# One row table with whole rows for chunks 0 to 7, its first read free of the later scatters, and counts in four steps a phase

## The chip, the core and the metric

The kernel runs on one core of a Trainium2 chip. The metric is the time of one execution in microseconds (us) on the device, the median over several runs. A profiled execution gives the trace; its own time and its span are in the table below.

## What is computed

Three stages follow one another on 1536 tokens of 512 features: a linear attention with decay, a dense MLP, and a mixture of eight experts. The change touches the last one, whose routing gives every token to exactly one expert, with at most 192 tokens an expert:

```python
cap = N // E                      # 1536 // 8 = 192
order = np.argsort(-(x @ w_gate).flatten())
for idx in order:                 # best (token, expert) pair first
    tok, e = divmod(int(idx), E)
    if assigned[tok] >= 0 or counts[e] >= cap:
        continue
    assigned[tok] = e; counts[e] += 1
for e in range(E):
    mask = assigned == e
    out[mask] = np.maximum(x[mask] @ w1[e], 0.0) @ w2[e]
```

## The kernel before

**Tiling.** The tokens are 12 chunks of 128. A product in float32 quality is three fp16 products of high and low parts. TensorE (PE) computes the MLP's second product `x2p` chunk by chunk (L647): 48 matmuls a chunk, 512 columns wide for chunks 0 to 7 and 384 wide for chunks 8 to 11. The last 128 columns of chunks 8 to 11 come later in one piece, `x2q` (L682), and are turned back by PE transposes `x2t` (L691).

**Routing** needs no x2, only logits, and runs beside that work. It takes seven phases (loop from L759). In a phase PE transposes the tokens' current best logits into a row of 1536 values (L767), ACT copies it to SBUF (L769), and for every chunk i a 0/1 matrix G (128 tokens by 1536) says which tokens are ahead of which: VectorE (DVE) writes the part left of the diagonal (L800) and the part right of it (L809); for chunks 8 to 11 ACT writes the left part in two passes (L803, L806). PE then counts with 32-column weights, four matmuls of 384 columns side by side for a chunk (`count`, L825 to L829, matmuls at L828): two chunks in a step, six steps a phase, in the order 0 1, 2 11, 3 4, 10 5, 9 6, 8 7. Ahead of the last step twelve `ties` matmuls (L792) use the same 32-column weights; their 0/1 inputs come from GpSimd (POOL, L775, L777) and DVE (L782). DVE thresholds the counts (L839), PE sums flags (L846, L847), and DVE settles the phase and makes the next logits (L737 to L752).

**Rows out and back in.** After the phases DVE writes every token's slot `pos` (L865). POOL scatters the x2 rows to DRAM, sorted by expert, with indirect DMAs, each of 128 rows: 12 into `xsa` (768 fp16 values a row, features 0 to 383 as high and low parts) and 12 into `xsb` (288 values a row: features 384 to 511, then the token's number and zeros); all at L881. Three of the `xsb` scatters stand among the first 12, nine behind them. A `memset` of a spare word (L879) separates scatters into one table. The SBUF copies are `xa` (three tiles of four chunks, pool B) and `xb` (one tile, pool B; a copy and a memset on POOL, L667 and L668, write the numbers and zeros). SP then reads the rows of two experts at a time with transposing DMAs, `xs<-xsa` (L903) and `xs<-xsb` (L904), and the numbers with four small DMAs (L909, L910). PE's first expert product `hp` (L928) takes features 0 to 383 of experts 0 and 1 first and their last 128 features after that; `po` (L958) is the second product.

**Order.** `Plan` writes the order by hand: `add` gives a step an engine, a planned cost, what it waits for, its buffers and a key; `run` (L96) simulates five engines and a shared DMA with these costs and emits the steps in the order of planned time, the lowest key first among those ready. So each engine's order is fixed ahead, and `x2p` matmuls (each a step of its own) fill PE wherever nothing with a lower key is ready in the plan. On the chip an engine runs its list in that order and waits where the data is late. Pool B has 21 buffers of 8 KB a partition, H has 2 of 4 KB, and the G tiles of chunks 8 to 11 take their buffers from H. Loads of expert weights (`ws`, L981) go through SP too, behind the row reads in its list.

Of the kernel before, what the change touches and what calls it, by code (L numbers as in the profile page):

```python
# [26 lines left out]
XA = 768  # L27
XB = 288
# [20 lines left out]
class Plan:  # L49
# [16 lines left out]
    def buf(self, pool, shape, dt, name):  # L66
        return Buf(self, pool, shape, dt, name)
# [28 lines left out]
    def run(self):  # L96
# [14 lines left out]
        while avail:  # L111
# [81 lines left out]
def fused_kernel(ctx, tc, raw_d, lam_d, win_d, wout_d, wg_d, w1_d, w2_d, out):  # L193
# [23 lines left out]
    def C(shape, dt, name):  # L217
        return cst.tile(shape, dt, name=name)
# [417 lines left out]
    xbb = buf("B", [P, NCH, XB], F16, "xb")  # L636

    def x2_part(j, d0, d1, pool, key):
        n = d1 - d0
        ps = buf(pool, [P, n // P, P], F32, f"x2p{j}_{d0}")  # L640
        prev = None
        for fc in range(16):
            w, w_done = wout[fc // 4]

            for y, z in ((0, 0), (0, 1), (1, 0)):
                def mm(fc=fc, w=w, y=y, z=z):
                    te.matmul(ps[:], gsl(y, fc, j), w[:, z, fc % 4, d0:d1], start=(fc + y + z == 0), stop=(fc == 15 and y == 1))  # L647
# [3 lines left out]
        parts = ([(xab[j // 4], t_xa, d0 // P, a)] if d0 < 384 else []) + ([(xbb, t_xb, b - 3, 1)] if d1 > 384 else [])  # L651
        if n == 512:
            parts = [(xab[j // 4], t_xa, 0, 3), (xbb, t_xb, 0, 1)]
        k0 = 0
        for x, done, ka, kb in parts:
            def v(y, x=x, ka=ka, kb=kb):
                return x[:, j if x is xbb else j % 4, 2 * P * ka:2 * P * kb].rearrange("p (k y d) -> p y k d", y=2, d=P)[:, y]
            src = slice(k0, k0 + kb - ka)
            k0 += kb - ka
            sc = 2.0 ** -9 / 6.0  # L660
            h = add("se", c_se((kb - ka) * P), lambda v=v, src=src: se.activation(v(0), ps[:, src], AF.Copy, scale=sc), [prev], [x, ps], key)
            lo = add("ve", c_ve((kb - ka) * P), lambda v=v, src=src: ve.scalar_tensor_tensor(
                v(1), ps[:, src], sc, v(0), op0=OP.mult, op1=OP.subtract), [h], [x, ps], key)
            done[j] = [lo]
            if x is xbb and j == 0:
                def tail():
                    ge.tensor_copy(xbb[:, :, 256:258].bitcast(I32), ids.unsqueeze(2))  # L667
                    ge.memset(xbb[:, :, 258:], 0.0)  # L668
                ids_in.append(add("ge", 0.4, tail, [prev], [x], key))
    for j in range(NCH):  # L670
        if j % 4 == 0:
            xab[j // 4] = buf("B", [P, 4, XA], F16, f"xa_{j}")
        x2_part(j, 0, 512 if j < JB else 384, "pB" if j % 3 == 2 else "pC", x_key + 11 * j)

    def x2_rest(b, key):
# [17 lines left out]
        r = slice(4 * b, 4 * b + 4)  # L693
        h = add("se", c_se(512), lambda: se.activation(xbb[:, r, 0:P], pt[:], AF.Copy), [t], [xbb, pt], GK)
        lo = add("ve", c_ve(512), lambda: ve.tensor_tensor(xbb[:, r, P:2 * P], pt[:], xbb[:, r, 0:P], op=OP.subtract), [h], [xbb, pt], GK)
        for j in range(4 * b, 4 * b + 4):
            t_xb[j] = [lo]
    x2_rest(2, x_key + 11 * NCH + 24)
    t_x2 = [t_xb[j] if j < JB else t_xa[j] for j in range(NCH)]

# [13 lines left out]
    pos = C([P, NCH], I32, "pos")  # L714
# [5 lines left out]
    BY_GE = 8  # L720

# [37 lines left out]
    for p in range(PHASES):  # L759
# [33 lines left out]
        order_c = [0, 1, 2, 11, 3, 4, 10, 5, 9, 6, 8, 7]  # L793
        group, t_g = [], []
        for n, i in enumerate(order_c):
# [26 lines left out]
            if len(group) < 2:  # L822
                continue

            def count(group=group, n=n, cp=cp):  # L825
                for i, z, G in group:
                    for k in range(4):
                        te.matmul(cp[32 * k:32 * k + 32, :], ohc[:, i], G[:, z, 384 * k:384 * k + 384], start=(n == 1 and i == group[0][0]),  # L828
                                  stop=(n == NCH - 1 and i == group[1][0]))  # L829
# [45 lines left out]
    last_to = []  # L875

    def scatter(dst, idx, src, done):
        if last_to[-1:] == [id(done)]:
            ge.memset(spare, 0.0)  # L879
        last_to.append(id(done))  # L880
        s = ge.indirect_dma_start(out=dst, out_offset=bass.IndirectOffsetOnAxis(ap=idx, axis=0), in_=src, in_offset=None)  # L881
        for o in done:
            tc.declare_no_dep(s.ins, o.ins, reason="distinct rows")
        done.append(s)
    sca, scb = [], []
    t_sa = [add("ge", 1.28, lambda j=j: scatter(xsa_d[:, :], pos[:, j:j + 1], xab[j // 4][:, j % 4], sca),
                [t_pos] + t_xa[j], [xab[j // 4]], GK + j, 0, 2 * P * XA) for j in range(NCH)]

    t_sb = [add("ge", 1.28, lambda j=j: scatter(xsb_d[:, :], pos[:, j:j + 1], xbb[:, j], scb),
                [t_pos] + t_xb[j] + ids_in + ([t_sa[3 * j + 2]] if j < 3 else t_sa[-1:]), [xbb], GK + (3 * j + 2.5 if j < 3 else NCH + j), 0, 2 * P * XB)  # L890
# [4 lines left out]
    xs, t_xs = {}, {}  # L895
    h1, t_h1 = {}, {}
    l1_first = {}

    def experts_in(q, key):
        xs[q] = buf("B", [P, 8, 2 * CAP], F16, f"xs{q}")  # L900
        r = slice(2 * CAP * q, 2 * CAP * q + 2 * CAP)
        first = [l1_first[2 * q - 2]] if q else []
        t_xs[q] = [add("sp", 4.7 if q else 2.4, lambda: sy.dma_start_transpose(out=xs[q][:, 0:6], in_=xsa_d[r, :]), t_sa + first, [xs[q]], key, 0, 725000),  # L903
                   add("sp", 1.25, lambda: sy.dma_start_transpose(out=xs[q][:, 6:8], in_=xsb_d[r, 0:256]), t_sb + first, [xs[q]], key, 0, 242000)]  # L904

    def load_rows():
        v = xsb_d[:, 256:258].bitcast(I32).rearrange("(q z c) o -> z c q o", z=2, c=CAP)
# [140 lines left out]
```

## Time and profile before

| | |
|---|---|
| median of 3 runs | 508.85 us (508.14 to 509.87) |
| the profiled execution | 508.18 us, span 506.3 us |
| mean granted TensorE clock | 0.992 of full speed |
| PE busy | 484.0 us, 96% of the span |
| DVE, ACT, POOL busy | 398.6, 309.1, 166.4 us |

Times in the rows below are microseconds from the span's start. The 2 us between the profiled execution's time and its span lie outside the first and last instruction. A row of a timeline reads: start, duration, engine, line of the kernel, operation, written tile and what it is made from, shape, how many merged, and in brackets the idle time of the engine just before and what ended it. Neighbouring matmuls overlap in the pipeline, so the time that one costs is read from start to start.

### The profile page before, as it was taken

The numbers are of one execution on the slowest core, as the hardware profiler recorded it, in microseconds if no ns is written. First come the engines' busy times: TensorE is split into PE (matmuls) and PEld (weight loads), VectorE is DVE, ScalarE is ACT, GpSimd is POOL, SyncE is SP. The second block draws the span as 40 slices with busy tenths as digits, with TensorE's granted clock in tenths as the row PEclk, the third lists the DMA queues.
The fourth block names the chain that finished last, engine by engine and source line by source line (L and its number), as shares of the span: only waits on it lengthen the run. The fifth ranks groups of instructions, "written<-read, shape, count | busy, mean of one in ns | idle before, by whom it ended". The sixth has DMA issues, their size and how long they took to land.

```text
span 506.3 us, 10304 instructions
## 1 busy us (share of the span) xinstructions
PE 484.0 (96%) x4241; PEld 294.2 (58%) x4243; DVE 398.6 (79%) x707; ACT 309.1 (61%) x486; POOL 166.4 (33%) x167
## 2 busy tenths in 40 slices
PE   8779998999999999999999999999999999999995
PEld 3467554787785444534434434546577685776862
DVE  7699999988688886598899889887644797989620
ACT  1586959764546664286687568574523758687510
POOL 2022334020222220076257347436880232323201
PEclk9898999999999999999999999999999999999999
DMA  7999426220264541000000000655665999998011
GB/s 225 398 415 411 179 84 247 85 43 2 84 250 85 99 89 22 2 2 1 1 1 2 1 0 1 250 201 189 225 142 176 370 285 423 320 399 358 1 43 41
DMA packets 44910, 77.86 MB, mean 154 GB/s; under 512 B 33080, under 2 KB 34112, under 8 KB 38720
## 3 DMA queue, kind: packets, MB, share of 16 engines
q1 hardware_dynamic: 42752, 70.82, 41.5%
q0 software_dynamic: 2112, 6.39, 3.4%
q8 instruction: 33, 0.54, 0.4%
q14 instruction: 13, 0.11, 0.1%
HBM read 63.46 MB, written 6.40 MB: 138 GB/s over the span
## 4 chain that ended last, share of the span: by engine, by line
PE 35%; DVE 35%; issue 9%; ACT 8%; DMA 7%; POOL 5%; POOLq 0%; SPq 0%; DVEq 0%; ACTq 0%
PE x2p L647 11%; DVE G L809 7%; PE hp L928 6%; PE po L958 6%; DVE G L800 3%; DVE r L536 3%; DMA ws<-w 3%; DVE g L416 3%; POOL xsb L881 2%; PE h L221 2%; ACT kd L439 2%; DMA raw<-raw 2%; PE h L223 2%; PE h L222 2%; DVE sm L458 2%
## 5 line engine op out<-in xcount | busy, mean ns | idle before, releaser
L647 PE MATMUL x2p<-wo,g 128*128 128x512 f16 (+1 forms) x576 | 124.6, 362 | 0.0
L221 PE MATMUL h<-xT,wi 128*128 128x256 f16 (+2 forms) x304 | 89.4, 303 | 1.8 <-DVE r L536 1.8
L222 PE MATMUL h<-xT,wi 128*128 128x256 f16 (+2 forms) x304 | 89.3, 303 | 0.0
L223 PE MATMUL h<-xT,wi 128*128 128x256 f16 (+2 forms) x304 | 89.3, 303 | 0.0
L647 PEld LDWEIGHTS <-g 128*128 128x128 f16 x576 | 52.6, 99 | 55.5 <-issue 10.5
L775 POOL TENSOR_SCALAR eq<-mrow,m 128x128 bf16<-128x128 f32 x56 | 56.7, 1030 | 84.8 <-DVE on L748 52.1
L416 DVE SCALAR_TENSOR_TENSOR w<-ws,w 128x1024 f16<-128x1024 f32 x58 | 71.3, 1272 | 11.8 <-ACT w L406 10.1
L406 ACT ACTIVATE w<-ws 128x1024 f16<-128x1024 f32 x64 | 64.5, 1050 | 10.2 <-DMA ws<-w 7.8
L928 PE MATMUL hp<-xs,w 128*128 128x192 f16 x768 | 65.2, 246 | 0.3 <-DMA xs<-xsb 0.3
L928 PEld LDWEIGHTS <-w 128*128 128x128 f16 x768 | 63.2, 98 | 3.7 <-issue 2.1
L958 PE MATMUL po<-w,h 128*64 128x512 f16 (+1 forms) x384 | 64.1, 380 | 0.1
L809 DVE TENSOR_SCALAR G<-mrow,m 128x1408 bf16<-128x1408 f32 (+10 forms) x77 | 52.0, 706 | 0.0
L385 POOL TENSOR_SCALAR wod<-wod 128x1024 f32<-128x1024 f32 x8 | 22.5, 2817 | 89.3 <-ACT wod L383 75.5
L406 ACT ACTIVATE g<-r 128x512 f16<-128x512 f32 (+1 forms) x52 | 30.7, 594 | 29.7 <-DVE r L536 28.8
L958 PEld LDWEIGHTS <-h 128*64 128x64 f16 (+1 forms) x384 | 29.0, 104 | 31.8 <-issue 1.7
L416 DVE SCALAR_TENSOR_TENSOR g<-r,g 128x512 f16<-128x512 f32 (+1 forms) x52 | 34.5, 666 | 11.3 <-ACT g L406 10.8
L536 DVE SCALAR_TENSOR_TENSOR r<-r,h 128x512 f32<-128x512 f32 (+1 forms) x52 | 33.1, 640 | 9.6 <-ACT r L535 9.3
L803 ACT ACTIVATE G<-mrow,m 128x1536 bf16<-128x1536 f32 (+3 forms) x28 | 39.4, 1407 | 0.8
L535 ACT ACTIVATE r<-h,c 128x512 f32<-128x512 f32 (+1 forms) x52 | 33.5, 644 | 10.2 <-PE h L223 10.0
L221 PEld LDWEIGHTS <-wi 128*128 128x128 f16 x304 | 30.0, 99 | 15.1 <-issue 1.6
L222 PEld LDWEIGHTS <-wi 128*128 128x128 f16 x304 | 30.1, 99 | 14.8 <-issue 2.1
L223 PEld LDWEIGHTS <-wi 128*128 128x128 f16 x304 | 30.1, 99 | 14.7
(154 smaller groups left out, 683.2 us busy)
## 6 DMA issues: line engine op xcount, KB each, us to landing
ws<-w SPq DMA_DIRECT2D x32, 1024.0 KB, 11.1
raw<-raw SPq DMA_DIRECT2D x24, 512.0 KB, 10.0
wis<-w_in SPq DMA_DIRECT2D x8, 1024.0 KB, 13.8
wos<-w_out SPq DMA_DIRECT2D x8, 1024.0 KB, 7.9
tab<-tz SPq DMA_DIRECT2D x1, 512.0 KB, 6.8
wt<-wo SPq DMA_TRANSPOSE x16, 3.2
xsa<-xa,pos POOLq DMA_INDIRECT x12, 4.1
xsb<-xb,pos POOLq DMA_INDIRECT x12, 3.5
```

Source lines behind the costliest of these rows:

```text
L221: te.matmul(ps, lh, rh, start=start, stop=False)
L222: te.matmul(ps, lh, rl, start=False, stop=False)
L223: te.matmul(ps, ll, rh, start=False, stop=stop)
L406: h = add("se", c_se(n), lambda: se.activation(dst()[0], src(), AF.Copy, scale=sc), deps, bufs, key, reserve)
L416: lo = add("ve", c_ve(n), lambda: ve.scalar_tensor_tensor(dst()[1], src(), sc, dst()[0], op0=OP.mult, op1=OP.subtract), [h], bufs, key)
L536: t = add("ve", c_ve(nf * T), lambda: ve.scalar_tensor_tensor(r[:], r[:], 6.0 * 2.0 ** -11, ps[:], op0=OP.min, op1=OP.mult), [t], [ps, r], ...
L647: te.matmul(ps[:], gsl(y, fc, j), w[:, z, fc % 4, d0:d1], start=(fc + y + z == 0), stop=(fc == 15 and y == 1))
L775: t_eq.append(add("ge", 1.06, lambda i=i, eq=eqs[0], mrow=mrow: ge.tensor_scalar(eq[:, i], mrow[:, P * i:P * i + P], m[:, i:i + 1], None, ...
L803: se.activation(G[:, z, 0:o], mrow[:, 0:o], AF.Sign, scale=-1.0, bias=m[:, i:i + 1])
L809: ve.tensor_scalar(G[:, z, o:], mrow[:, o:], m[:, i:i + 1], None, op0=OP.is_le)
L928: te.matmul(ps[:, i], w[:, z, kk % 2, cl], x[:, 2 * kk + y, CAP * i0:CAP * i0 + CAP], start=(i + kk + y + z == 0), stop=(i == 1 and kk == ...
L958: te.matmul(o, h1[e][:, y, k, cl], w2[e, fh][0][:, zz, f], start=(k + y + zz == 0), stop=(k == 7 and y == 1))
```

## The change

- One DRAM table `xs_d`, 2304 values (4608 bytes) a row, takes the place of `xsa` and `xsb`. Chunks 0 to 7 go out whole, 1152 values a row, in one scatter each; chunks 8 to 11 go out in two, 768 values and later 384. That is 8 + 4 + 4 = 16 scatters. Three index tiles (`pos`, `pos3`, `pos6`) replace one.
- The SBUF rows of chunks 0 to 7 are three tiles of up to three chunks, each with a copy and a memset of its own for numbers and zeros; the last block of chunks 8 to 11 has a tile in pool H, taken once `x2q` is done, with such a tail too. The result of a whole chunk leaves PSUM in one ACT and one DVE instruction, not two each.
- The four late scatters are declared free of the first two experts' first read, and are planned behind its issue. The other experts' first reads are not named there. The plan's cost of a scatter's DMA becomes a fixed 1.6 us.
- A phase counts in four steps: 0 1 2 11, 3 4 10 5, 9 6, 8 7; a step of four chunks is planned at 0.78 us, one of two stays at 0.44 us.

```diff
-XA = 768
-XB = 288
+XA, XB, XW, XS = 768, 384, 1152, 2304
...
-            if s.nbytes:
+            if s.nbytes < 0:
+                s.on, s.end = "dma", s.end + 1.6
+            elif s.nbytes:
...
-    xbb = buf("B", [P, NCH, XB], F16, "xb")
+    xbb = buf("H", [P, NCH - JB, XB], F16, "xb")
+    ids_all = []
...
+        x, z = row_at[j]
+        def v(y):
+            return x[:, z, 0:2 * n].rearrange("p (k y d) -> p y k d", y=2, d=P)[:, y]
+        sc = 2.0 ** -9 / 6.0
+        h = add("se", c_se(n), lambda: se.activation(v(0), ps[:], AF.Copy, scale=sc), [prev], [x, ps], key)
+        t_xa[j] = [add("ve", c_ve(n), lambda: ve.scalar_tensor_tensor(
+            v(1), ps[:], sc, v(0), op0=OP.mult, op1=OP.subtract), [h], [x, ps], key)]
+        if n == 512 and z == 0:
+            def tail():
+                k = min(3, JB - j)
+                ge.tensor_copy(x[:, 0:k, 1024:1026].bitcast(I32), ids[:, j:j + k].unsqueeze(2))
+                ge.memset(x[:, 0:k, 1026:], 0.0)
+            ids_all.append(add("ge", 0.4, tail, [prev], [x], key))
...
+    BATCHES = [[0, 1, 2, 11], [3, 4, 10, 5], [9, 6], [8, 7]]
...
-            if len(group) < 2:
+            if i not in [b[-1] for b in BATCHES]:
                 continue
...
-            t_c = add("pe", 0.44, count, t_g + [t_c, t_oh], [x[2] for x in group] + [cp], GK)
+            t_c = add("pe", 0.1 + 0.17 * len(group), count, t_g + [t_c, t_oh], [x[2] for x in group] + [cp], GK)
...
-        ve.tensor_copy(pos, vm)
+        ve.tensor_scalar(pos, vm, XS // XW, None, op0=OP.mult)
+        ve.tensor_scalar(pos3, vm, XS // XA, None, op0=OP.mult)
+        ve.tensor_scalar(pos6, vm, XS // XB, XA // XB, op0=OP.mult, op1=OP.add)
...
-    xsa_d = dram.tile([NCH * P, XA], F16, name="xsa")
-    xsb_d = dram.tile([NCH * P, XB], F16, name="xsb")
+    xs_d = dram.tile([NCH * P, XS], F16, name="xs_d")
...
+    def scatter(dst, idx, src, done, clear=()):
+        ge.memset(spare, 0.0)
         s = ge.indirect_dma_start(out=dst, out_offset=bass.IndirectOffsetOnAxis(ap=idx, axis=0), in_=src, in_offset=None)
+        for o in [*done, *clear]:
+            tc.declare_no_dep(s.ins, o.ins, reason="distinct rows or columns")
         done.append(s)
+    sc_x, early_reads = [], []
+
+    def rows_out(j, x, z, w, idx, deps, key, clear=()):
+        return add("ge", 1.28, lambda: scatter(xs_d[:, :].rearrange("n (t w) -> (n t) w", w=w), idx[:, j:j + 1], x[:, z], sc_x, clear),
+                   [t_pos] + deps, [x], key, 0, -1)
+    t_sa = [rows_out(j, *row_at[j], XW if j < JB else XA, pos if j < JB else pos3, t_xa[j] + (ids_all if j < JB else []), GK + j)
             for j in range(NCH)]
...
+    def early(ld, q):
+        if q == 0:
+            early_reads.append(ld)
...
+        t = add("sp", 4.7 if q else 2.4, lambda: early(sy.dma_start_transpose(out=xs[q][:, 0:6], in_=xs_d[r, 0:XA]), q), t_sa + first, [xs[q]], key, 0, 725000)
+        if q == 0:
+            issued = add("sp", 0.0, lambda: None, t_sa, [], key)
+            t_sb.extend(rows_out(j, xbb, j - JB, XB, pos6, t_xb[j] + ids_in + [issued], GK + NCH + j, early_reads) for j in range(JB, NCH))
+        t_xs[q] = [t, add("sp", 1.25, lambda: sy.dma_start_transpose(out=xs[q][:, 6:8], in_=xs_d[r, XA:XA + 256]), t_sb + first, [xs[q]], key, 0, 242000)]
...
```

## Rows read from the trace of the kernel before

**Rows 1.** Busy time by stretch: window, length, engines (instructions), granted clock, DMA share, GB/s
```profile
254.00:272.00 18.00, 17.66 (x135) 7.79 (x134) 16.68 (x43) 12.95 (x14) 9.27 (x10) 1.00 0.01 1
...
362.00:382.00 20.00, 19.31 (x164) 14.09 (x163) 9.86 (x9) 8.01 (x10) 16.17 (x22) 1.00 0.48 127
382.00:389.00 7.00, 6.54 (x78) 6.25 (x76) 2.90 (x8) 3.48 (x8) 0.00 (x0) 1.00 0.53 100
389.00:468.00 79.00, 78.99 (x682) 55.03 (x683) 68.40 (x82) 59.27 (x76) 22.05 (x20) 1.00 1.02 363
468.00:500.50 32.50, 32.33 (x282) 21.13 (x278) 11.18 (x19) 10.22 (x16) 5.45 (x8) 1.00 0.07 25
```

**Rows 2.** Timeline of PE in the third phase
```profile
256.83 1.90 PE L647 MATMUL x2p<-wo,g 128*128 128x512 f16 x8
258.66 0.51 PE L828 MATMUL cp<-G,ohc 128*32 128x384 bf16 x8
259.10 1.04 PE L647 MATMUL x2p<-wo,g 128*128 128x512 f16 x4
260.07 0.50 PE L828 MATMUL cp<-G,ohc 128*32 128x384 bf16 x6
260.91 0.34 PE L828 MATMUL cp<-G,ohc 128*32 128x384 bf16 x2 [0.34 <-DVE G L809]
261.18 1.04 PE L647 MATMUL x2p<-wo,g 128*128 128x512 f16 x4
262.15 0.51 PE L828 MATMUL cp<-G,ohc 128*32 128x384 bf16 x8
262.48 0.34 PE L792 MATMUL cp<-eq,ohc 128*32 128x128 bf16 x12
```

**Rows 3.** Waits over the whole span: who for whom, us in total, times, longest
```profile
PE cp L828 <- DVE G L809: 2.5, 7, 0.5
```

**Rows 4.** Timeline of DVE in the same phase
```profile
259.42 1.69 DVE L809 TENSOR_SCALAR G<-mrow,m 128x768 bf16<-128x768 f32 x2
...
261.63 0.87 DVE L809 TENSOR_SCALAR G<-mrow,m 128x640 bf16<-128x640 f32 x2
```

**Rows 5.** Timeline of PE where the experts begin
```profile
371.88 0.66 PE L691 MATMUL x2t<-ident,xq 128*128 128x128 f32 x4 [0.69 <-ACT xq L686]
372.38 12.04 PE L928 MATMUL hp<-xs,w 128*128 128x192 f16 x144
384.74 4.12 PE L928 MATMUL hp<-xs,w 128*128 128x192 f16 x48 [0.32 <-DMA xs<-xsb]
```

**Rows 6.** Timeline of POOL, scatters: first and last of xsa, last four of xsb begin and end
```profile
344.67 1.92 POOL L881 DMA_INDIRECT xsa<-xa,pos  x1 [11.54 <-DVE pos L865]
...
363.23 1.17 POOL L881 DMA_INDIRECT xsa<-xa,pos  x1 [0.19 <-issue]
...
375.17 1.43 POOL L881 DMA_INDIRECT xsb<-xb,pos  x1 [0.19 <-issue]
...
379.43 0.96 POOL L881 DMA_INDIRECT xsb<-xb,pos  x1 [0.19 <-issue]
```

**Rows 7.** Line L903, 368.4 to 372 us: the first two reads' issue on SP, and landing
```profile
L903 SPq DMA_TRANSPOSE xs<-xsa x2: 2409/2614/2819, 366.1 to 368.6; - x2
...
DMA to landing us min/median/max: 5.1/5.3/5.6
```

**Rows 8.** Timeline of DVE: the slots, the last rows of x2, the last block
```profile
344.20 0.17 DVE L865 CAST pos<-vm 128x12 int32<-128x12 f32 x1
...
361.40 0.56 DVE L662 SCALAR_TENSOR_TENSOR xa<-x2p,xa 128x384 f16<-128x384 f32 x1 [4.50 <-ACT xa L661]
...
373.95 0.68 DVE L695 TENSOR_TENSOR xb<-x2t,xb 128x512 f16<-128x512 f32 x1
```

**Rows 9.** Chain that ended last, 379 to 390 us: the first read of xsb
```profile
381.71 2.99 DMA xs<-xsb
```

**Rows 10.** Groups of POOL: the tail that writes the numbers (busy us, mean ns)
```profile
L667 POOL COPY xb<-ids 128x12 int32<-128x12 int32 x1 | 0.6, 587 | 0.0
```

More of the change, by code (lines that the diff above doesn't have):

```diff
@@ L650, in x2_part @@
         a, b = min(d1, 384) // P, max(d0, 384) // P
[L651 to L669, printed above, removed]
@@ new lines, in x2_part @@
+        if n == 512 and z == 0:
[4 more added lines that the diff above has]
+            ids_all.append(add("ge", 0.4, tail, [prev], [x], key))
+    row_at = {}
+    for j in range(NCH):
+        if j < JB and j % 3 == 0:
+            row_at[j] = buf("B", [P, 3, XW], F16, f"xa_{j}"), 0
+        elif j == JB:
+            row_at[j] = buf("B", [P, NCH - JB, XA], F16, f"xa_{j}"), 0
+        else:
+            row_at[j] = row_at[j - 1][0], row_at[j - 1][1] + 1
@@ L697, in x2_rest, with tail @@
             t_xb[j] = [lo]
+        def tail():
+            ge.tensor_copy(xbb[:, :, 256:258].bitcast(I32), ids[:, JB:].unsqueeze(2))
+            ge.memset(xbb[:, :, 258:], 0.0)
+        ids_in.append(add("ge", 0.4, tail, [prev], [xbb], GK))
     x2_rest(2, x_key + 11 * NCH + 24)
-    t_x2 = [t_xb[j] if j < JB else t_xa[j] for j in range(NCH)]
+    t_x2 = t_xa
     A = C([P, NCH, NE], BF, "A")
@@ L713, in fused_kernel @@
     ohc = C([P, NCH, 32], BF, "ohc")
-    pos = C([P, NCH], I32, "pos")
+    pos, pos3, pos6 = (C([P, NCH], I32, n) for n in ("pos", "pos3", "pos6"))
     ge.memset(ohc, 0.0)
@@ L792, in ties @@
                     te.matmul(cp[32 * k:32 * k + 32, P * f:P * f + P], ohc[:, b], eqs[b >= BY_GE][:, b % BY_GE], start=False, stop=False)
[L793 removed]
         group, t_g = [], []
[L795 removed]
+        for n, i in enumerate(sum(BATCHES, [])):
             G, z = (Gs[i // 2], i % 2) if i < BY_SE else (Gs[i - BY_SE // 2], 0)
@@ L821, in fused_kernel, with count @@
             t_g += t
-            if len(group) < 2:
+            if i not in [b[-1] for b in BATCHES]:
                 continue
-            def count(group=group, n=n, cp=cp):
+            def count(group=group, cp=cp):
                 for i, z, G in group:
                     for k in range(4):
-                        te.matmul(cp[32 * k:32 * k + 32, :], ohc[:, i], G[:, z, 384 * k:384 * k + 384], start=(n == 1 and i == group[0][0]),
-                                  stop=(n == NCH - 1 and i == group[1][0]))
+                        te.matmul(cp[32 * k:32 * k + 32, :], ohc[:, i], G[:, z, 384 * k:384 * k + 384], start=(i == BATCHES[0][0]),
+                                  stop=(i == BATCHES[-1][-1]))
             if n == NCH - 1:
                 t_c = add("pe", 0.2, ties, [t_c, *t_eq], eqs + [cp], GK)
-            t_c = add("pe", 0.44, count, t_g + [t_c, t_oh], [x[2] for x in group] + [cp], GK)
+            t_c = add("pe", 0.1 + 0.17 * len(group), count, t_g + [t_c, t_oh], [x[2] for x in group] + [cp], GK)
             group, t_g = [], []
@@ L902, in experts_in @@
         first = [l1_first[2 * q - 2]] if q else []
-        t_xs[q] = [add("sp", 4.7 if q else 2.4, lambda: sy.dma_start_transpose(out=xs[q][:, 0:6], in_=xsa_d[r, :]), t_sa + first, [xs[q]], key, 0, 725000),
-                   add("sp", 1.25, lambda: sy.dma_start_transpose(out=xs[q][:, 6:8], in_=xsb_d[r, 0:256]), t_sb + first, [xs[q]], key, 0, 242000)]
+        t = add("sp", 4.7 if q else 2.4, lambda: early(sy.dma_start_transpose(out=xs[q][:, 0:6], in_=xs_d[r, 0:XA]), q), t_sa + first, [xs[q]], key, 0, 725000)
[3 more added lines that the diff above has]
+        t_xs[q] = [t, add("sp", 1.25, lambda: sy.dma_start_transpose(out=xs[q][:, 6:8], in_=xs_d[r, XA:XA + 256]), t_sb + first, [xs[q]], key, 0, 242000)]
     def load_rows():
-        v = xsb_d[:, 256:258].bitcast(I32).rearrange("(q z c) o -> z c q o", z=2, c=CAP)
+        v = xs_d[:, XA + 256:XA + 258].bitcast(I32).rearrange("(q z c) o -> z c q o", z=2, c=CAP)
         for z in range(2):
```

17 lines of the change are left out of this document (2 added, 15 removed).

## The prediction

> **What bounds the kernel now.** I read the busy time by stretch first. From the middle of routing to the last matmul PE is almost never idle, at a granted clock of 1.00: 17.66 us of the 18 us around one phase, 19.31 of 20 where the rows go out, 78.99 of 79 and 32.33 of 32.5 in the experts [rows 1]. So the end is set by how much PE has to do plus the little it waits, and a shorter chain on POOL, DVE, SP or the DMA is worth only the wait that it removes. What is left of idle time is in two places: a wait in every phase for DVE's G [rows 2, 3], and one where the second half of `hp` waits for the read of `xsb`, 0.32 us [rows 5]. The 0.69 us ahead of `x2t` [rows 5] is PE waiting for ACT, which the change leaves alone. I then read PE's timeline of a phase from start to start, because merged busy times hide what a change of tile shape costs, and last POOL's, SP's and DVE's timelines around the scatters, to see how far they are from holding PE up.
>
> **Counts in four steps.** The number of count matmuls stays; four steps in place of six remove two entries into the 128x32 shape and two exits a phase. Their price comes from [rows 2]. A run of eight `x2p` matmuls takes 258.66 - 256.83 = 1.83 us to the next block, a run of four 260.07 - 259.10 = 0.97 us: four matmuls cost 0.86, 0.215 each, and every run carries 0.11 us more. Eight count matmuls that are followed by `x2p` take 259.10 - 258.66 = 0.44 us; eight followed by `ties`, which keep the shape, take 262.48 - 262.15 = 0.33. So leaving costs 0.11 too. Rounding pulls both up a little; I take 0.2 us for an entry and exit. Two a phase in seven phases: 14 x 0.2 = 2.8 us less work on PE.
>
> **What the phase takes back.** PE's list is in order, and a phase is paced by DVE (16.68 of 18 us [rows 1]), so I follow the waits. Now the step 10 5 starts at 260.07 and its end waits for chunk 5's G: it lasts until 261.18, 1.11 us and not 0.44, so 0.67 us are lost; the pair of DVE instructions that it needs starts at 259.42 [rows 2, 4]. The profile counts half of that as idle, seven times in all [rows 3]. In the step 3 4 10 5 eight more matmuls (0.33 us) lie ahead of chunk 5's, but PE also comes there about 0.2 us sooner, two switches having gone: some 0.5 us stay lost. Behind it the plan now books 0.78 us where it booked 0.44, so one or two of the four `x2p` matmuls at 261.18 go elsewhere and PE reaches 9 6 some 0.3 us before 262.15. There chunk 6's right part is not done: it is the first of the two DVE instructions from 261.63 on that last 0.87 us together [rows 4], so it ends near 262.2. That is a new wait of 0.3 to 0.4 us. Per phase 0.67 us lost become 0.5 + 0.35 = 0.85, about 0.2 more: 7 x 0.2 = 1.4 us given back. The plan says the same: it books 2 x (0.88 - 0.78) = 0.2 us less a phase, one `x2p` matmul of 0.215 us more, 1.5 us in seven phases. Net 2.8 - 1.4 = **1.4 us** gained. The ends: everything given back, 0; or nothing new, and the old wait shorter by the 0.33 us of two more chunks, 2.8 + 7 x 0.33 = 5.1. I take 1.4, since plan and waits agree on it.
>
> **First read and scatters.** First the twelve scatters. Before, 14 (two of `xsb` among them) start between 344.67 and 363.23 [rows 6], 18.56 / 13 = 1.43 us apart. Twelve alone would put the last at 344.67 + 11 x 1.43 = 360.4. It also needs chunk 11's rows, at 361.96 now [rows 8] and 1.4 us sooner with PE: 360.6. With some 0.2 us to issue, 360.8. Before, the read followed 366.1 - 363.2 = 2.8 us behind [rows 6, 7]; now at 363.6, and with 5.1 us to land [rows 7] it is there at 368.7. PE wants it at 372.38 - 1.4 = 371.0 [rows 5]: 2.3 us to spare, where it was 366.05 + 5.1 = 371.2 against 372.38. So the earlier read is worth **nothing**: `x2p` and `x2q` cover it. A whole row is 1.5 times the bytes of one of `xsa`; issue does not follow bytes (0.96 us is the common length of a scatter of either table on POOL, the row at 379.43 being one). More bytes can only show in landing, for which there are the 2.3 us.
>
> Then the four late scatters. Their block is ready at 373.95 + 0.68 = 374.6 [rows 8], 373.2 now. POOL is free by then; starting at 373.4 and spaced as before (375.17 to 379.43, 4.26 us for three steps [rows 6]) the last starts at 377.7, lands after 381.71 - 379.43 = 2.28 us and is read in 2.99 [rows 9]: 383.0. PE ends the first half of `hp` at 371.0 + 12.04 = 383.0. The wait of 0.32 us goes: **0.3 us**. What is late next is the same read, with nothing in hand.
>
> One wait is added: experts 2 and 3's first read is of the same table and stands ahead of the late scatters in the plan, and only experts 0 and 1's is declared free. It follows 2.6 us behind on SP and lands after 5.6 [rows 7]: 363.6 + 2.6 + 5.6 = 371.8, before 373.2. So it costs 0, with 1.4 us in hand; behind the waiting scatter on POOL stand only the other three, and behind them on SP the second read, the small reads and the next weights.
>
> **Small edits, at nothing.** Two more index instructions on DVE stand behind `pos` (0.17 us each [rows 8]); the first eight scatters need only `pos`. The tails on POOL become four, smaller than the one that takes 0.6 us plus its memset [rows 10]; POOL is busy 9.27 of 18 us in a phase [rows 1]; if that cover were gone they would cost under 3 us once. A whole chunk's DVE result costs about 0.68 us (512 columns) and no longer 0.56 plus one of 128 columns [rows 8]: a gain on DVE, not on PE. The H buffer is taken after the last G. The freed B buffer lets no weight load pass the reads, since those of experts 2 to 7 are planned behind them. In the experts PE waits for nothing [rows 1], and their loads move up with the reads.
>
> **Sum.** 508.18 - 1.4 - 0.3 = 506.5 us for the profiled execution (span 504.6). That execution lies 0.67 us under the median of its kernel, so the median forecast is 507.1; rounded toward the larger end of the first term, **507.0**.
>
> The Trainium skill, "DMA: Bandwidth & Descriptors", section on the anatomy of one DMA, gives each transfer a fixed cost of about 2.0 us. By it eight scatters fewer would be an estimated 16 us; here scatters start 1.43 us apart and PE is busy meanwhile [rows 1, 6], so the trace puts them at nothing.
>
> **Rivals.** First, all comes back as waiting: DVE sets each phase, PE only arrives sooner. For it: DVE's share of a phase. Against: PE has `x2p` left behind the phases, so the plan can fill. Gain 0.3 us, 508.5.
>
> Second, the waits shrink as well: 5.1 + 0.3 us, 503.4. For it: two chunks more ahead of chunk 5's matmuls. Against: the arithmetic at 9 6 above.
>
> Third, on the other side, slower reads: rows of the first read are 1536 of 4608 bytes, no longer a whole row of their table. If a read takes 1.5 times as long, the first lands at 371.3, 0.3 us late, and the next one at 371.8 + 2.6 + 1.4 = 375.8 (half of 5.1 behind the first, and half of its own 2.8 spacing); the late scatters wait 2.6 us and so does `hp`. 508.85 - 1.7 + 2.6 = 509.7. It decides from reads about 1 us longer each, where the 1.4 us are used up, and the total is slower than before from about 1.4 times. Against it: the read of `xsb` already took 256 of 288 values a row, and a third of the data took 2.99 us against 5.1 [rows 7, 9], so no loss by pitch shows there. The same page's section on latency and other measured facts puts a transposing read with a non-contiguous middle dimension at 261 GB/s against 350 to 400, some 1.4 times; no row of this case shows that loss.
>
> **How the numbers follow.** The forecast has 0.47, the first rival 0.25, the second 0.10, slower reads 0.13, and 0.05 is for a plan that shifts for other reasons. A measurement can tell about 0.3%, 1.5 us, from no change. The forecast lies just beyond: of its 0.47 I count 0.38 as faster; with the second rival and a little of the rest 0.50. Same: 0.25 plus 0.09, 0.35. Slower 0.15. The range goes from 504.0, most of the way to the second rival, to 509.7, the third.
>
> **What would show it.** Right: four count blocks a phase, a block of 16 of about 0.77 us, an `x2p` matmul more in each phase, a wait at 9 6 beside the one at chunk 5; `xs_d` scatters 16, the first read issued near 363.6 and landed before `x2q` ends; no wait ahead of `hp`'s second half. Wrong: PE idle ahead of the first `hp`, late scatters that wait on a DMA, reads above 6.5 us, or phases that last clearly longer than the 18 us of now.

## The result, and the profile after

The change made the kernel slower: 514.6 us median of 4 runs (514.04 to 515.84) beside 509.36 of 4 runs of before, a ratio of 1.0108 [1.0085, 1.0131]. A second measurement (r12 below) gave 515.01 beside 508.40, 1.0122 [1.0102, 1.0142]. The forecast was 507.0, and its range ended at 509.7. The profiled execution took 515.84 us (span 514.1, mean granted clock 0.985) where that of before took 508.18 (506.3, 0.992). These two are 7.7 us apart and the medians 5.2 and 6.6, because the profiled execution of the change was the slowest of its four and that of before close to its fastest; what follows accounts for the pair of profiles.

PE's busy time by stretch, columns as in [rows 1], with one phase, the stretch in which the rows go out, and three behind it:

```profile
254.00:272.00 18.00, 17.58 (x136) 8.23 (x135) 16.83 (x42) 12.76 (x13) 9.95 (x11) 1.00 0.01 2
...
362.00:382.00 20.00, 17.79 (x139) 13.26 (x138) 6.58 (x7) 4.91 (x6) 3.93 (x6) 0.91 0.52 137
382.00:389.00 7.00, 3.75 (x46) 3.60 (x44) 0.00 (x0) 0.00 (x0) 3.23 (x6) 1.00 0.16 52
389.00:421.00 32.00, 30.66 (x240) 21.25 (x239) 25.20 (x36) 21.43 (x29) 4.50 (x5) 0.89 0.99 307
```

The phase is as full as in [rows 1]. From 362 us on it is not: 17.79 us of 20 at a granted clock of 0.91 (19.31 before), 3.75 of 7 (6.54 before), and a clock of 0.89 behind that. So the loss lies between 362 and about 397 us. PE's timeline there, against [rows 5]:

```profile
370.00 0.66 PE L694 MATMUL x2t<-ident,xq 128*128 128x128 f32 x4 [0.69 <-ACT xq L689]
372.18 13.57 PE L942 MATMUL hp<-xs,w 128*128 128x192 f16 x144 [1.52 <-DMA xs<-xs_d]
390.19 6.84 PE L942 MATMUL hp<-xs,w 128*128 128x192 f16 x48 [4.44 <-DMA xs<-xs_d]
397.18 3.18 PE L972 MATMUL po<-w,h 128*128 128x512 f16 x14
```

PE comes to `x2t` 1.88 us sooner than before (371.88) and to `po` 8.2 us later (389.01 in the trace of before, right behind the last `hp` of [rows 5]). Four pieces turn the 1.88 us of lead into 8.2 of delay. `hp` waits 1.52 us for the first read. Its first half takes 13.57 us for 12.04. Its second half then waits 4.44 us for the second read, where it waited 0.32, and takes 6.84 for 4.12. From the start of `po` on nothing more is lost: it runs 110.9 us from its first to its last matmul, before 111.0. The two longer halves are the same matmuls at a lower clock, as the windows around them show (the granted clock is the third number from the end):

```profile
372.00:376.00 4.00, 3.82 (x28) 3.66 (x28) 0.02 (x1) 0.00 (x0) 1.10 (x2) 0.58 0.07 25
376.00:386.00 10.00, 9.75 (x119) 9.60 (x117) 0.00 (x0) 0.00 (x0) 3.23 (x6) 1.00 0.36 80
386.00:390.00 4.00, 0.00 (x0) 0.00 (x0) 0.00 (x0) 0.00 (x0) 0.00 (x0) 0.88 0.31 74
390.00:397.00 7.00, 6.81 (x48) 6.25 (x48) 4.90 (x12) 3.31 (x7) 0.00 (x0) 0.58 0.78 228
```

PE is busy 3.82 of 4 us from 372 on, yet does 28 matmuls, where 10 us at full clock hold 119. The mean of 0.58 is most of the stretch at the lower level, 1.2 GHz, and the rest at 2.4.

**Why the second half waits.** The chain that ended last, from 372.8 us on, and POOL's timeline of the same time:

```profile
372.79 2.35 DMA xs_d<-xb,pos
...
375.21 6.24 DMA xs<-xs_d
...
382.21 0.96 POOL xs_d L887
...
384.75 2.32 DMA xs_d<-xb,pos
...
387.09 3.06 DMA xs<-xs_d
```

```profile
360.83 0.96 POOL L887 DMA_INDIRECT xs_d<-xa,pos  x1 [0.19 <-issue]
...
362.10 1.99 POOL L887 DMA_INDIRECT xs_d<-xa,pos  x1 [0.19 <-issue]
...
372.79 0.99 POOL L887 DMA_INDIRECT xs_d<-xb,pos  x1 [7.86 <-issue]
...
382.21 0.96 POOL L887 DMA_INDIRECT xs_d<-xb,pos  x1 [8.32 <-DMA xs<-xs_d]
```

Only the first of the four late scatters goes out at once. The first read of experts 2 and 3 stands behind it in the order and waits until it has landed (372.79 + 2.35 = 375.14); it takes 6.24 us, and the other three scatters wait for it, 8.32 us on POOL. Only then can they, and the second read of experts 0 and 1, go. Two waits stand in a row, each a whole transfer long, between the block's first scatter and the read that `hp` wants.

**Why the first half waits.** What SP waits for between 345 and 395 us, and line L914 (the first reads) between 367 and 370 us:

```profile
SPq L995 <- DMA xs_d<-xa,pos: 11.2, 1, 11.2
...
SPq L914 <- DMA xs_d<-xa,pos: 6.0, 1, 6.0
```

```profile
L914 SPq DMA_TRANSPOSE xs<-xs_d x1: 2560/2560/2560, 367.5 to 367.5; - x1
...
DMA to landing us min/median/max: 4.6/4.6/4.6
```

A weight load (L995) waits 11.2 us for scatters, and the first read stands behind it on SP. The load is the last of expert 1, a megabyte; it takes a buffer of pool B that held rows which two of the scatters send out. It is issued at 361.1 us, when the last two of the twelve scatters are going out. These take 6.1 and 5.4 us to land, where [rows 6, 7] give 2.8 us from the last scatter to the read's issue. The read waits for them from 361.5 on (6.0 us) and not for the load itself: what delays it is the load's megabyte moving beside the last scatters. It is issued at 367.5, not at 363.6, and there at 372.1. PE had come at 370.5.

### The profile page after: what moved, and what is told of

Same layout as the page of the kernel before. It is cut to its first block, busy times and chain, and to the rows that moved or that the text cites. A ratio compares the mean times of both kernels' runs of the same rounds, so it can differ in the third digit from the quotient of the medians.

```text
span 514.1 us, 10280 instructions
## 1 busy us (share of the span) xinstructions
PE 485.5 (94%) x4241; PEld 298.5 (58%) x4243; DVE 398.9 (78%) x701; ACT 309.0 (60%) x478; POOL 159.5 (31%) x164
## 4 chain that ended last, share of the span: by engine, by line
DVE 36%; PE 35%; issue 11%; ACT 8%; DMA 6%; POOL 2%; POOLq 0%; ACTq 0%; DVEq 0%; SPq 0%
PE x2p L650 10%; DVE G L818 7%; PE hp L942 7%; PE po L972 7%; DVE G L809 4%; DVE r L538 3%; DVE g L418 3%; ACT kd L441 2%; DVE sm L460 2%; PE h L223 2%; DMA xs<-xs_d 2%; PE h L225 2%; PE h L224 2%; DVE eq L792 2%; PE cp L837 2%
## 5 line engine op out<-in xcount | busy, mean ns | idle before, releaser
L650 PE MATMUL x2p<-wo,g 128*128 128x512 f16 (+1 forms) x576 | 122.4, 362 | 0.0
L223 PE MATMUL h<-xT,wi 128*128 128x256 f16 (+2 forms) x304 | 88.4, 301 | 2.8 <-DVE r L538 2.8
L225 PE MATMUL h<-xT,wi 128*128 128x256 f16 (+2 forms) x304 | 88.3, 300 | 0.0
L224 PE MATMUL h<-xT,wi 128*128 128x256 f16 (+2 forms) x304 | 88.3, 300 | 0.0
L650 PEld LDWEIGHTS <-g 128*128 128x128 f16 x576 | 53.7, 99 | 54.4 <-issue 6.4
L942 PE MATMUL hp<-xs,w 128*128 128x192 f16 x768 | 69.5, 255 | 6.0 <-DMA xs<-xs_d 6.0
L942 PEld LDWEIGHTS <-w 128*128 128x128 f16 x768 | 66.8, 101 | 10.1 <-issue 7.5
L948 ACT ACTIVATE rr<-hp 128x384 f32<-128x384 f32 x32 | 15.6, 490 | 43.7 <-PE hp L942 43.5
L410 DVE TENSOR_SCALAR h<-rr 128x384 f16<-128x384 f32 x32 | 13.9, 434 | 33.3 <-ACT rr L948 33.1
L224 PEld LDWEIGHTS <-wi 128*128 128x128 f16 x304 | 29.7, 98 | 15.9 <-issue 3.2
```

The lines of the kernel that those rows point to most:

```text
L223: te.matmul(ps, lh, rh, start=start, stop=False)
L224: te.matmul(ps, lh, rl, start=False, stop=False)
L225: te.matmul(ps, ll, rh, start=False, stop=stop)
L942: te.matmul(ps[:, i], w[:, z, kk % 2, cl], x[:, 2 * kk + y, CAP * i0:CAP * i0 + CAP], start=(i + kk + y + z == 0), stop=(i == 1 and kk == ...
```

## The experiments

The table is worked out from the profiled executions. "Routing" runs from the first weight load of `x2p` to the first of `x2q`; "to the end" from the former to the start of the last `po` matmul (0.1 us each). The idle columns are what `hp` of experts 0 and 1 waits for its two reads. The medians of before differed from chip to chip (508.40 to 511.52 us), so ratios of different chips are compared with that in mind; runs r1 to r4, r5 to r8 and r9 to r12 each share a chip. The last three columns are of one execution each, and not always of a typical one: that of r4 was the slowest of its ten, that of r7 the fastest. The two kernels with two profiles (the change and r12, r2 and r9) agree within 0.2 us in both sums.

| run | ratio to before | median us | routing | to the end | idle ahead of first, second half |
|---|---|---|---|---|---|
| before | 1 | 508.4 to 511.5 | 157.4 | 296.9 | 0, 0.32 |
| the change | 1.0108 [1.0085, 1.0131] | 514.60 | 155.9 | 305.4 | 1.52, 4.44 |
| r1 reads free | 0.9975 [0.9947, 1.0004] | 509.26 | 155.8 | 298.9 | 2.34, 0 |
| r2 free, load behind | 0.9915 [0.9886, 0.9944] | 506.99 | 155.8 | 295.2 | 0, 0.24 |
| r3 before, four steps | 1.0015 [0.9981, 1.0049] | 511.73 | 155.1 | 299.9 | 2.17, 0 |
| r4 reads planned behind | 0.9948 [0.9919, 0.9978] | 508.37 | 155.8 | 300.9 | 1.71, 0 |
| r5 load behind alone | 1.0061 [1.0028, 1.0095] | 514.83 | 155.9 | 302.6 | 0, 5.57 |
| r6 six steps | 1.0038 [1.0001, 1.0075] | 515.22 | 157.2 | 305.0 | 3.76, 2.30 |
| r7 two tables, four steps, `xsa` first | 1.0009 [0.9970, 1.0048] | 512.15 | 154.7 | 296.6 | 0, 1.10 |
| r8 before, `xsa` first | 1.0064 [1.0040, 1.0089] | 515.30 | 157.4 | 303.5 | 0, 0 |
| r9 r2 again | 0.9933 [0.9917, 0.9948] | 505.41 | 155.9 | 295.3 | 0, 0.31 |
| r10 planned behind, load behind | 1.0009 [0.9989, 1.0030] | 508.29 | 155.9 | 296.8 | 0, 0.29 |
| r11 r9 with six steps | 1.0061 [1.0042, 1.0080] | 511.42 | 157.4 | 300.2 | 0, 2.92 |
| r12 the change again | 1.0122 [1.0102, 1.0142] | 515.01 | 155.9 | 305.2 | 1.67, 4.26 |

### r1: every first read free of the late scatters

No instruction moves; what goes is that read and scatter wait for each other, in both directions.

```diff
     def early(ld, q):
-        if q == 0:
-            early_reads.append(ld)
+        for o in sc_x[NCH:]:
+            tc.declare_no_dep(ld.ins, o.ins, reason="distinct columns")
+        early_reads.append(ld)
```

> The changed kernel with every first read (columns 0 to 767) declared free of the late scatters, both ways; no instruction moves. Order theory (the first read of experts 2 and 3 stands between the first late scatter and the other three, waits for the one and makes the three wait): the four late scatters start one behind the other, about 372.8 to 377 us, the wait of 4.4 us ahead of hp's second half goes and with it the half clock behind it (2.7 us): about 507.5 us, under 509. The wait of 1.5 us ahead of the first hp stays. Rival (a read of rows 4608 bytes apart, or whole rows, are slow in themselves): the wait ahead of the second half stays above 2 us, 512 us or more.

Measured: 509.26 us, 0.9975; to the end it is 305.4 - 298.9 = 6.5 us less than the change. PE's timeline where the experts begin:

```profile
373.46 17.65 PE L943 MATMUL hp<-xs,w 128*128 128x192 f16 x192 [2.34 <-DMA xs<-xs_d]
391.25 5.99 PE L973 MATMUL po<-w,h 128*128 128x512 f16 x27
```

Both halves run through without a wait between them; the four late scatters start at 373.25, 374.54, 375.80 and 377.07. So the second wait was the order of read and late scatters and nothing else. The first wait is still there (2.34 us; the read is issued at 368.08 behind the load).

### r2: and the weight load behind the first read

```diff
-               lambda i: t_x2[[8, 8, 8, 8, 9, 9, 9, 10][4 * e + i]] if e < 2 else t_xs[0][1:])
+               lambda i: t_xs[0][:1] if 4 * e + i == 7 else t_x2[[8, 8, 8, 8, 9, 9, 9, 10][4 * e + i]] if e < 2 else t_xs[0][1:])
```

> The kernel of r1_free, and the last weight load of expert 1 planned behind the first read in SP's list, not ahead of it. Load theory (that load waits for a buffer that a scatter frees, its 1 MB runs beside the last two scatters, and the first read waits for both): the last scatters land within 3 us and not 5.4 to 6.1, the first read is issued near 364 us and not at 367.5, no wait ahead of the first hp and no half clock there: 1.5 + 1.5 us less than r1_free, about 505 us. Rival (the last scatters land late because whole rows still fill the rings): they land as late as in the changed kernel, and the time is that of r1_free.

Measured: 506.99 us, 2.3 less than r1 on the same chip, and faster than before. SP's timeline, then PE's:

```profile
364.91 2.38 SPq L915 DMA_TRANSPOSE xs<-xs_d  x1
367.38 0.53 SPq L996 DMA_DIRECT2D ws<-w  x1
368.00 4.83 SPq L915 DMA_TRANSPOSE xs<-xs_d  x1
```

```profile
370.68 12.04 PE L943 MATMUL hp<-xs,w 128*128 128x192 f16 x144
382.96 4.12 PE L943 MATMUL hp<-xs,w 128*128 128x192 f16 x48 [0.24 <-DMA xs<-xs_d]
```

The first read goes out at 364.9 (368.08 in r1), `hp` follows `x2t` without a wait, both halves have the length of [rows 5], and what is left is the 0.24 us wait that before had as 0.32.

### r3: the counts alone, in the kernel before

```diff
-        order_c = [0, 1, 2, 11, 3, 4, 10, 5, 9, 6, 8, 7]
+        BATCHES = [[0, 1, 2, 11], [3, 4, 10, 5], [9, 6], [8, 7]]
+        order_c = sum(BATCHES, [])
...
-            t_c = add("pe", 0.44, count, t_g + [t_c, t_oh], [x[2] for x in group] + [cp], GK)
+            t_c = add("pe", 0.1 + 0.17 * len(group), count, t_g + [t_c, t_oh], [x[2] for x in group] + [cp], GK)
```

> The kernel before with counts in four steps alone. The prediction's first term: 1.4 us less than before (0.997), x2t starts at about 370.4 us; measured by x2t in the changed kernel it would be 1.9 us. Rival (all comes back as waits in the phases): within 0.5 us of before, x2t at 371.4 or later.

Measured: no difference from before (1.0015). Routing is 2.3 us shorter, and `hp` gives it back:

```profile
370.31 0.66 PE L691 MATMUL x2t<-ident,xq 128*128 128x128 f32 x4 [0.69 <-ACT xq L686]
373.13 6.27 PE L929 MATMUL hp<-xs,w 128*128 128x192 f16 x54 [2.17 <-DMA xs<-xsa]
```

Before had 1.2 us between the landing of its first read and PE's coming ([rows 5, 7]); the counts used that up and more, the read was issued no sooner (367.50, before 366.05), and the idle time was followed by a stretch at the lower clock. A gain ahead of a transfer with little in hand turned into a wait.

### r4: the first reads of experts 2 to 7 planned behind the late scatters

```diff
-        t = add("sp", 4.7 if q else 2.4, lambda: early(...), t_sa + first, [xs[q]], key, 0, 725000)
+        t = add("sp", 4.7 if q else 2.4, lambda: early(...), t_sa + (t_sb if q else []) + first, [xs[q]], key, 0, 725000)
```

> The changed kernel with the first reads of experts 2 to 7 planned behind the four late scatters, nothing declared free beyond the change. Order theory: the late scatters run one behind the other as in r1_free and the time is within 1 us of it (about 507.5), because the second read is needed only some 15 us later. Rival (slow table): 512 us or more, as in the changed kernel.

Measured: 508.37 us, beside 509.26 of r1. The late scatters start in a row (373.89 to 377.71) and the second half has no wait, as in r1, this time by order alone; the first wait stays at 1.71 us. The profiled execution took 512.58 us, and some of that is a new loss behind it, which comes back in r10: PE waits for cast weights in the experts, three times (us in total, times, longest).

```profile
PE hp L942 <- DVE w L418: 2.1, 3, 0.8
```

### r5: the weight load alone

The edit of r2, without that of r1.

> The change with one edit alone: the last weight load of expert 1 is planned behind the first read of experts 0 and 1 (in r2 this came together with the second first read freed of the late scatters). Theory (two separate costs): with the load gone from beside them the last two of the twelve scatters land about 3 us sooner, the first read is issued at about 365 us, and hp starts with no wait of its own (0 to 0.4 us, where the change had 1.52); but the second first read still stands between the first late scatter and the other three, so the second half of hp still waits several us for xs<-xs_d (3.5 to 5.5, the change had 4.44), with a stretch of granted clock 0.5 around it. Time between the change and r2: 511 to 512.5 us. Rival (one cause, the order of read and late scatters makes both waits): the first wait stays near 1.5 us and the time stays at the change's 514.6. Second rival (the load makes both waits): the second half waits under 1 us and the time is r2's 507.

Measured: 514.83 us, 1.0061; the waits are those of the theory, the time is some 2 us above the one that it gave. PE's timeline:

```profile
370.04 12.04 PE L942 MATMUL hp<-xs,w 128*128 128x192 f16 x144
387.65 6.13 PE L942 MATMUL hp<-xs,w 128*128 128x192 f16 x48 [5.57 <-DMA xs<-xs_d]
```

The first wait and its slow stretch are gone, and the second wait stays, a little longer (5.57 us): each wait has its own cause. What the first cost is seen less clearly: to the end it is 305.4 - 302.6 = 2.8 us in the profile, the ratio is lower than the change's, and the median is not (it was taken on a chip where before had 511.52).

### r6: the counts back to six steps

```diff
-    BATCHES = [[0, 1, 2, 11], [3, 4, 10, 5], [9, 6], [8, 7]]
+    BATCHES = [[0, 1], [2, 11], [3, 4], [10, 5], [9, 6], [8, 7]]
```

> The change with its counts taken back to six steps a phase; the table, the sixteen scatters and the reads stay. Theory: the counts' own worth is about 2 us of TensorE work in the phases, and the loss of the change lies in the two waits for reads; so x2t comes about 2 us later (near 372), the first wait of hp shrinks from 1.52 us to about nothing or a few tenths and the wait at the second half of hp stays at 3 to 5 us: time within 1 us of the change, 513.5 to 515.5. Rival (the counts in four steps are themselves the loss, through blocks of counts that keep the chain of selection waiting): the time falls to 509 or less. Second rival (the gain of the counts is fully kept in the changed kernel): the time rises to 516.5.

Measured: 515.22 us, the time that the theory gave, but not in its way. With six steps the plan put 36 matmuls of `hp` ahead of the last of `x2q` and of `x2t`, so PE came to the first read sooner and waited 3.76 us. By the ratio (1.0038) it is nearer to before than the change was, on another chip. Routing is 157.2 us as in before, so 1.3 us are the counts'; the rest of this run decides nothing.

### r7 and r8: the scatters of `xsa` first, in the two tables of before

r8 is before with one edit, r7 adds the counts of r3.

```diff
-                [t_pos] + t_xb[j] + ids_in + ([t_sa[3 * j + 2]] if j < 3 else t_sa[-1:]), [xbb], GK + (3 * j + 2.5 if j < 3 else NCH + j), 0, 2 * P * XB)
+                [t_pos] + t_xb[j] + ids_in + t_sa[-1:], [xbb], GK + NCH + j, 0, 2 * P * XB)
```

> The kernel before (24 scatters, two tables) with the counts in four steps and with all twelve scatters of the first table ahead of the first scatter of the second. Theory: the counts' gain of about 2 us in the phases was swallowed in r3 by the wait of hp for the first read, whose last source scatter was queued behind scatters of the second table; with that scatter 2 to 3 us sooner the first read is issued at about 364 to 365 us, hp does not wait, no stretch of granted clock 0.5 stands there, and the gain shows: ratio to before 0.994 to 0.998 (508 to 510 us beside a before of 511). The first-half wait may go and a wait at the second half come: its scatters now all stand last, as nine in a row from about 364 to 375, and they were the last to land in before as well. Rival (the counts' gain never reaches the end, whatever the reads): ratio 1.000 to 1.002, as r3. Second rival (the later scatters of the second table delay the second read): a wait of 1 us or more at the second half of hp, ratio above 1.002.

> The kernel before with one edit alone: all twelve scatters of the first table ahead of the first scatter of the second. Theory: before, the first read had landed ahead of hp, and the wait of hp's second half was 0.3 us; a read that lands sooner changes nothing, so ratio 0.998 to 1.002. Rival (the read's place is worth something by itself, whatever the counts): ratio under 0.997. Second rival (nine scatters of the second table in a row land later): wait at the second half of hp of 1 us or more, ratio above 1.002.

Measured: r8 was slower than before, 1.0064, where the theory gave no difference: the size of its second rival without that rival's cause, since the second half of `hp` does not wait. r7 was equal to before, 1.0009, where the theory gave 0.994 to 0.998, with runs from 506.79 (the profiled one) to 516.01, and waits 1.10 us there. Neither waits for its first read. PE's timeline of r8 shows another loss:

```profile
374.16 4.70 PE L928 MATMUL hp<-xs,w 128*128 128x192 f16 x55
379.16 0.58 PE L928 MATMUL hp<-xs,w 128*128 128x192 f16 x5 [0.31 <-issue]
380.63 0.49 PE L928 MATMUL hp<-xs,w 128*128 128x192 f16 x4 [0.88 <-issue]
```

and so on until 385 us: 3.2 us idle in six pieces for which the profile names no releaser, while twelve small scatters in a row go out (366.2 to 382.5). Behind these pieces the granted clock is 0.50 (384 to 388 us) and 0.80 (388 to 392), and from `hp`'s start to `po` r8 takes 6.6 us longer than before: 3.2 idle, the rest slow. r7 and r3 have 1.2 and 1.3 us of the same in three pieces. The changed kernel and its variants have none, before has none. What holds PE there stays open. What follows is weak: r7 less r8 is 0.55% with intervals that overlap, a sign and no proof that counts in four steps pay where no read is waited for; and r7's profiled execution, its fastest, comes near r9's with all 24 scatters (296.6 and 295.3 us to the end), which its median does not.

### r9 to r12 on one chip: the pair again, its two halves, and the change

r9 is r2 and r12 is the change, both without a further edit.

> The kernel of r2 again (the change with every first read free of the late scatters and the last load of expert 1 behind the first read), beside r10, r11 and r12 on one chip. Theory (both waits gone, the counts' gain kept): ratio to before 0.989 to 0.994, no wait of hp above 0.5 us and granted clock full from 364 to 390 us. Rival (r2 was a favourable chip): ratio above 0.997.

> The change itself, beside r9 to r11 on one chip, so that its distance to them does not rest on two chips. Theory: ratio to before 1.008 to 1.013 as first measured, and the same two waits of hp (1 to 2 us and 4 to 5 us), each with a stretch of granted clock 0.5 behind it. Rival (the loss differs by chip): ratio under 1.006.

Measured: 505.41 us (504.83 to 506.24) against 515.01. Two edits that take no work away are worth 9.6 us. The pair is 3.0 us faster than before on this chip (508.40), 0.9933 [0.9917, 0.9948], as r2 was; the change loses as it did on the first chip.

r10 is r4's edit with r2's, so no read is declared free.

> The change with two edits of the plan and no declaration: the first reads of experts 2 to 7 planned behind the four late scatters (as r4), and the last load of expert 1 behind the first read (as r5). Theory (the loss is where read and load stand in the order, not that the tracker counts the table as one): both waits of hp go, as in r9: ratio 0.989 to 0.995. The second first-read is then issued later than in r9, behind the last late scatter's landing near 376 to 380 us, and the second read behind it at 380 to 383 us, so up to 1 us of wait may stay at the second half of hp. Rival (the declaration itself is needed, since the wait on the table costs wherever the read stands): ratio above 0.998.

Measured: 508.29 us, 1.0009: the theory missed. Neither half of `hp` waits (0 and 0.29 us), so the order alone does remove both waits; but 3 us are lost elsewhere. SP's timeline of r10, then of r9:

```profile
383.22 1.53 SPq L995 DMA_DIRECT2D ws<-w  x3
384.84 9.65 SPq L914 DMA_TRANSPOSE xs<-xs_d  x1
...
395.91 0.52 SPq L995 DMA_DIRECT2D ws<-w  x1
```

```profile
368.47 4.80 SPq L915 DMA_TRANSPOSE xs<-xs_d  x1
...
384.33 1.55 SPq L996 DMA_DIRECT2D ws<-w  x3
...
387.61 5.02 SPq L996 DMA_DIRECT2D ws<-w  x3
```

In r9 the first read of experts 2 and 3 goes out in a free stretch, at 368.5. In r10 it takes SP 9.65 us at 384.8, where it stands ahead of the next weight loads, which start at 395.9 and not at 387.6. r10's profile shows PE waiting 0.8 us for a cast weight in `hp`, and r4's, with the same order of reads, 2.1 us in three waits; r9's and r1's show none. From the first `po` matmul to the last it is 112.5 us in r10 and 113.5 in r4, where r1 and r9 take 110.9. So 1.6 of the 3 us lie in the stretch that the late loads feed. The profiled execution of r10 is one of the two fastest of twelve (506.67 to 511.46) and shows no more; that the late loads are the whole of it is inferred.

r11 is r9 with the edit of r6.

> r9 with its counts taken back to six steps a phase, so the counts' worth is measured where no wait for a read stands behind them (r6 could not do this: there the plan put a part of hp ahead of the last matmuls of x2q, so TensorE came to its wait earlier). Theory: 14 mode changes fewer are worth about 2 us (1.4 forecast, 1.9 seen at x2t in the change), so this kernel is 1.5 to 2.5 us slower than r9: ratio to before 0.993 to 0.998. Rival (the counts' gain never reaches the end): equal to r9 within 0.5 us. Second rival (the counts are worth the whole of r9's gain of 4.3 us): ratio 1.000.

Measured: 511.42 us, 6.0 more than r9, where 1.5 to 2.5 were expected. Routing tells 157.4 - 155.9 = 1.5 us of it. The rest is in PE's timeline:

```profile
369.88 1.65 PE L943 MATMUL hp<-xs,w 128*128 128x192 f16 x18
371.37 0.38 PE L685 MATMUL x2q<-g,wo 128*128 128x512 f16 x1
...
373.07 0.60 PE L694 MATMUL x2t<-ident,xq 128*128 128x128 f32 x4
...
385.50 5.77 PE L943 MATMUL hp<-xs,w 128*128 128x192 f16 x48 [2.92 <-DMA xs<-xs_d]
```

As in r6 the plan moved a piece of `hp` ahead of `x2t`. So the last block, the late scatters (375.80 for 373.27) and the second read (382.54 for 380.31) come 2.2 to 2.5 us later, and the second half waits 2.92 us and runs slow (5.77 for 4.12). The counts' own price is the 1.5 us; the run also shows how little the second read has in hand.

## Why the prediction was wrong

**Counts and phases: right.** Forecast 2.8 us less work, 1.4 given back, net 1.4. Routing shrank from 157.4 to 155.9 us, 1.5. Both waits of a phase came where they were expected. PE in the third phase, against [rows 2]:

```profile
255.82 0.83 PE L837 MATMUL cp<-G,ohc 128*32 128x384 bf16 x16
...
259.28 0.83 PE L837 MATMUL cp<-G,ohc 128*32 128x384 bf16 x14
260.46 0.34 PE L837 MATMUL cp<-G,ohc 128*32 128x384 bf16 x2 [0.35 <-DVE G L818]
260.73 0.82 PE L650 MATMUL x2p<-wo,g 128*128 128x512 f16 x3
261.48 0.91 PE L837 MATMUL cp<-G,ohc 128*32 128x384 bf16 x8
262.06 0.50 PE L802 MATMUL cp<-eq,ohc 128*32 128x128 bf16 x12
```

The wait for chunk 5's G stays, 0.35 us idle: the step that ends with it lasts 260.73 - 259.28 = 1.45 us where 0.77 was said for its 16 matmuls, so 0.68 is lost and not 0.5. The step 9 6 takes 262.06 - 261.48 = 0.58 us to `ties` and not 0.33: the new wait, 0.25 where 0.3 to 0.4 was said. In the two-table kernels four steps were worth 2.3 us (r3) and 2.7 (r7); why more there was not tried.

**"One wait is added ... stands ahead of the late scatters in the plan ... costs 0": the step that failed.** The prediction had experts 2 and 3's first read ahead of all four late scatters, issued 2.6 us behind the first read and landed before the block was ready. In the trace it stands behind the first late scatter and ahead of the other three. Reads and writes of this table wait for each other in that order unless they are declared free, so both sides of the read became a wait. The step priced one direction, the scatters waiting for the read, and not the other. r1 takes these waits away without moving anything, and the kernel is 6.5 us shorter to the end; r4 removes them by order.

**"The freed B buffer lets no weight load pass the reads": also wrong.** It looked at the loads of experts 2 to 7. The last load of expert 1 stands ahead of the reads, and with the smaller row tiles it got a buffer that two scatters had to leave first. Its bytes moved beside the last scatters. Their late landing and 1.3 us from the scatters themselves (below) used up the 2.3 us to spare: issue 367.5, not 363.6. Moving the load was worth 2.3 us in the median (r1 to r2).

**The missing term.** Neither the sum nor a rival counted what PE does after it has waited. Partly at 1.2 GHz the two halves took 1.53 and 2.72 us longer, as much as the first idle time (1.52) and over half of the second (4.44). With the terms of this profile: 1.68 later from `x2t` to `hp`, 5.65 to the second half, 2.72 in it, less 1.88 that `x2t` came sooner, is 8.2, which is the distance of `po`. The Trainium skill, "TensorE: Matmul & The Clock Gate", section on HAM oscillation, describes PE's clock falling in a wait for a DMA, so that what follows starts slow. The windows of 372 to 376 and 390 to 397 us, both 0.58, agree.

**Mis-sized: twelve scatters.** They were to start 1.43 us apart and end at 360.4 to 360.8. They took (362.1 - 343.4) / 11 = 1.70 us each, in the change and in r2 alike, so the last of the twelve goes out 1.3 us later than said. "Issue does not follow bytes" holds: in the change the eight whole rows take 1.43 us on POOL on the mean and the four shorter ones 1.47, each from 0.96 to 1.99. But long ones are more frequent than before, and in r7 twelve `xsa` scatters, of the size of before, were 1.54 apart too. What makes one long stays open. In r2 the read goes out at 364.9 for that reason and is still in time.

**The term of 0.3 us did not come.** With both waits gone the second half of `hp` still waits 0.24 us (r2) and 0.31 (r9) for the same read, where before waited 0.32.

**Right:** reads from the wider table are not 1.5 times as long. The first takes 4.6 us (before 5.1) and 5.3 in r1, where the second follows at once as it did before; the second takes 6.2 (before 5.6), and in r9 6.9 beside a weight load, where PE doesn't need it yet. r2 and r9 lose nothing by them, so the third rival fell. Scatters by number are worth little as far as profiles tell: r7 with 24 comes within 1.3 us of r9 with 16, both to the end, though in r7's fastest execution. The Trainium skill, "DMA: Bandwidth & Descriptors", section on the anatomy of one DMA, states a fixed cost of about 2.0 us, from which the estimate of 16 us for eight fewer came; no run here shows such a price. Its section on latency and other measured facts states a loss for transposing reads with a non-contiguous middle dimension; no run here shows that loss. Two of the signs named for being wrong, "late scatters that wait on a DMA" and "PE idle ahead of the first `hp`", are what the profile shows. The small edits on DVE and POOL cost nothing that a row shows.

**The end on the other side** came by another mechanism than the rival that had it. With both waits gone the kernel is 296.9 - 295.2 = 1.7 us faster to the end (r2). That is the number of the forecast, 1.4 + 0.3, and in part by luck: routing gave 1.6 and the wait at the second half 0.1. By the medians it is more, 3.0 us (r9) to 4.0 (r2); that rest no pair of profiles shows.

## What to carry to other kernels

When several transfers are put into one table, write down for every pair of write and read in the emitted order who waits for whom, in both directions; a key or a planned time doesn't tell it, the order of the instructions does. Follow each freed or resized buffer to the next transfer that takes it, since that transfer inherits a wait, goes out later, and its bytes then move beside whatever else is on the way at that time. And price an idle stretch of PE with the slow stretch that may follow it: here waits of 1.5 and 4.4 us cost 1.5 and 2.7 us more, while pauses of 1.2 us in three pieces and a wait of 1.10 in r7 left the granted clock at 1.00.

## What the runs showed of the hardware

A transfer of a megabyte beside two scatters made these land in 6.1 and 5.4 us, where r9's last three took a median of 2.7 without it. In three kernels with ten or twelve small scatters in a row behind those that the first read waits for (r3, r7, r8), PE paused in `hp` with no wait that the profile names, 1.2 to 3.2 us in all; the kernel before, with the same scatters as r3, did not. In r8 the granted clock fell to 0.50 behind the pauses. What makes PE pause stays open.
